# k^T v of the fourth batch placed inside the last block of the second unit's second stage

## The chip, the cores and the metric

The kernel runs on one core of one Trainium2 chip. The time is the device time of that core in microseconds, the median of three runs. A profile comes from one further execution under the hardware profiler. In it PE is TensorE (PEld its weight loads), DVE is VectorE, ACT is ScalarE, POOL is GpSimd and SP is SyncE, which here only issues transfers.

## What is computed

Two stages of a network, one behind the other, in float32 (the weights arrive in a wider type and are folded to float32 on the chip):

```python
# q, k, v: (8 batches, 8 heads, 576, 64)
kv  = np.einsum('bhsd,bhse->bhde', k, v)
out = np.einsum('bhsd,bhde->bhse', q, kv)
rms = np.sqrt(np.mean(out * out, axis=-1, keepdims=True) + 1e-06)
x   = (out / rms * g_norm)            # then (B,H,S,D) -> (4608, 512)

# w_in: (512, 2048), w_out: (2048, 512)
h = x @ w_in
r = np.maximum(h, 0.0)
g = s * (r * r) + b
out = g @ w_out                       # (4608, 512)
```

## The kernel before

The 4608 rows are cut into 36 chunks of 128 rows and nine units of four chunks. A unit u goes through a first stage (x @ w_in, then the squared relu) and a second stage (g @ w_out). Both stages use Strassen-like schemes: seven products of halves in place of eight, with sums of the operands made by VectorE. They are named after the bank that they fill and their number: x1, z2, x6, y7, x5, x3, y4. From the third unit on (u = 2), part of the first stage is split once more; `small(i, pair, ...)` (line 882) are its quarter-size products.

Units count from 0 in the code, batches too. The "second unit" is u = 1, the "fourth batch" is b = 3.

Everything is in an order written out by hand: each engine runs its instructions in the order in which the Python code emits them, and waits only on semaphores for data and buffers. Attention of the next unit is laid between the products of the present one. It comes in steps: `turn` transposes q on VectorE, `product` multiplies it with `bd_kv`, `back`, `square`, `row_sum`, `norm` and `turn_x` finish it. `bd_kv` holds k^T v of two batches, one in each of two buffers (`bd_kv[b % 2]`).

`kv_product(b, beside)` (lines 365 to 400) makes k^T v of one batch: for each of two halves, nine steps of four 64x64 products (in the trace 144 matmuls in all), which fall into the four quadrants of the array; then ScalarE copies the results into `bd_kv[b % 2]`. With `beside` true the results go into one bank of the tag "z" and one of the tag "y" of the pool `ps_f`, which the unit's own products use as well. Without it they go into the two banks of the pool `ps_t` with the tag "t", in which attention's `product` writes.

The table `kv_due` says in which unit a batch's k^T v is made: b = 2 in u = 1, b = 3 in u = 2, b = 4 in u = 3 and so on. k and v of that batch come through a ring of 14 slots in SBUF, `w_sb`, that also carries the weights of the second stage and of the split first stage. `pump()` issues the next loads of one long list on SP's queue as long as slots are free; `used(...)` marks entries as read, frees the slots from the front of the list, and pumps. A load waits, on SP, until the last reader of its slot is done, and the loads behind it wait with it. At the end of u = 1 the list holds: the weights of products 5, 3 and 4 of its second stage (four slots each), then eight loads of k and v for u = 2 (line 114), ten loads of split weights for u = 2 (line 1075), and then the second stage's weights of u = 2 (line 1089).

The second stage of u = 1 is a list of 14 functions, `mm2(1)`, called in a loop (line 1814). Each is one product for one half of the rows; `product(i, j, ...)` (line 1113) runs eight blocks, one matmul of the program each; the trace records each float32 matmul as two, with a weight load each, so that the halves j = 0 and 1 together are 32 recorded 128x256 matmuls. The last two are y4(0) and y4(1). Behind each function run the steps that the dictionary of `side_of` (line 1628) names for its index: parts of the attention for u = 2, and loads of q.

The first stage of u = 2 is `run` in `mm1_deep(u)` (line 947). It calls `at(n)` between products; `sides(u, A, B)` (line 1728) says what stands at each n. Its beginning is:

```python
x1(0)
at(2)
x1(1)
sums_of_x()
small(2, 0, 1, 2)
x6(0)
at(4)
```

`at(2)` is the turn of q for the first attention pair (VectorE) and, in units 2 and 5, `kv_product` with `beside`. `at(4)` is that pair's `product` with `bd_kv`, the first reader of the fourth batch's k^T v. `sums_of_x` is four subtractions on VectorE. `small(2, 0, 1, 2)` is four matmuls into the bank of the tag "x" of `ps_a` (sx_ps) and four into a "z" bank.

Of the kernel before, what the change touches and what calls it, by code (L numbers as in the profile page):

```python
# [17 lines left out]
def kernel(  # L18
# [47 lines left out]
    NP = H // 2  # L66
    KC = DM // P
    FC = DF // P
# [22 lines left out]
    def matmul(o, lhsT, rhs, start, stop):  # L91
        nc.tensor.matmul(o, lhsT=lhsT, rhs=rhs, start=start, stop=stop, skip_group_check=True)  # L92
# [166 lines left out]
    def add(o, a, b):  # L259
        nc.vector.tensor_tensor(out=o, in0=a, in1=b, op=ALU.add)  # L260
# [98 lines left out]
    def warm(n):  # L359

        ps = ps_f.tile([P, 2, TB], FP32, name="warm_ps", tag="z", bufs=1)
        for _ in range(n):
            matmul(ps[:, 0, :P], ident, ident, True, True)

    def kv_product(b, beside=False):

        if beside:
            ps = [  # L370
                bank_of("kv", tag, bufs).rearrange("p b (m d) -> p (b m) d", d=D)[:, :2]
                for tag, bufs in (("z", 1), ("y", 2))
            ]
        else:
            ps = [ps_t.tile([P, 2, D], FP32, name="kv_ps", tag="t") for _ in range(2)]
        for i in range(2):
            if b == 0:
                warm((18, 7)[i])
            kv = [kv_in.pop((b, 2 * i + l)) for l in range(2)]
            for j in range(R):  # L380
                for l in range(2):
                    for r in range(2):
                        rows = slice(r * HB, r * HB + HB)
                        nc.tensor.matmul(  # L384
                            ps[r][(r ^ l) * HB : (r ^ l) * HB + HB, i, :],
                            lhsT=kv[l][0][rows, j, :],
                            rhs=kv[l][1][rows, j, :],
                            start=(j == 0),
                            stop=(j == R - 1),
                        )  # L390
        for r in range(2):
            rs = slice(r * HB, r * HB + HB)
            for l in range(2):
                cs = slice((r ^ l) * HB, (r ^ l) * HB + HB)
                to = bd_kv[b % 2][rs, l:NP:2, rs].rearrange("p i (c e) -> p i c e", c=KC)
                src = ps[r][cs].rearrange("p i (e c) -> p i c e", c=KC)
                if b == 0 and l == 1:
                    nc.vector.tensor_copy(out=to, in_=src)
                else:
                    nc.scalar.copy(to, src)  # L400
# [237 lines left out]
    def bank_of(key, tag, bufs=2):  # L638
        bank[key] = ps_f.tile([P, 2, TB], FP32, name=f"{tag}_ps", tag=tag, bufs=bufs)
        return bank[key]  # L640
# [407 lines left out]
    kv_due = {(b // 2 * R + b % 2 * 4) // 4 - 1: b for b in range(2, B)}  # L1048
# [43 lines left out]
    def used(*keys):  # L1092

        done.update(keys)
        while held and held[0] in done:
            held.pop(0)
        pump()
# [5 lines left out]
    def mm2(u, step=None, side={}):  # L1103
# [6 lines left out]

        st = {}

        def product(i, j, ps, first):
            for f in range(FC // 2):
                s, b = divmod(f, 2)
                w2 = W2_AT[i][:, f] if u == 0 else ring[u, i, f // 4][:, :, f % 4]
                matmul(
                    ps, ga[G_OF[i], s][:, b, j * P : j * P + P], w2,
                    first and f == 0, f == FC // 2 - 1,
                )  # L1120
            if u > 0 and j == 1:
                used((u, i, 0), (u, i, 1))

        def plus_of(o, ps, other, copy=nc.scalar.copy):
# [173 lines left out]
            plus_of(rows("o1", j)[:, HN:], st["x", j], None if u == 1 else st["o1", j][:, HN:])  # L1298
            store("o1", j, 4 * u + j)

        def y4(j):
            product(4, j, st["y", j], False)
            add(rows("o2", j)[:, :HN], st["y", j], st["r2", j])
            store("o2", j, 4 * u + 2 + j)

        def seq(fn, *more):
            def run():
                fn()
                for m in more:
                    m()  # L1310
            return run
# [28 lines left out]
        if u == 1:  # L1340
            return [
                seq(lambda: x1(0), lambda: parts_of_w(1)),
                seq(lambda: x1(1), s2),
                seq(lambda: z2(0), lambda: parts_of_w(2)),
                seq(lambda: z2(1), s4),
                seq(lambda: x6(0), lambda: parts_of_w(6)),
                lambda: x6(1),
                seq(lambda: y7(0), lambda: parts_of_w(7)),
                lambda: y7(1),
                seq(lambda: x5(0), lambda: parts_of_w(5)),  # L1350
                lambda: x5(1),
                seq(lambda: x3(0), lambda: parts_of_w(3)),
                lambda: x3(1),
                seq(lambda: y4(0), lambda: parts_of_w(4)),
                lambda: y4(1),
            ]

        def slot(j, k):
# [163 lines left out]
    blocks = [i for s in range(NS) for i in (2 * s, NU + 2 * s)]  # L1522
# [45 lines left out]
    turn, take, product, square, root, norm, turn_x = zip(*(attention(c) for c in range(4)))  # L1568
# [59 lines left out]
    def side_of(A, B, sums, u):  # L1628

        if u == 0:  # L1630
            return {
                6: [A["turn"], lambda: kv_product(1)],
                8: [A["product"], A["back"], A["square"]],
                9: [A["row_sum"], B["turn"]],
                10: [A["norm"], partial(loads, 2, 0), A["turn_x"], A["scale"], B["product"], B["back"], B["square"]],
                11: [B["row_sum"], B["norm"]],
                12: [B["turn_x"], B["scale"], lambda: [fn() for fn in sums_w_in(0)]],
                13: [sums],
            }
        pieces = []  # L1640

        def ask(n):
            if n == 0:
                pieces.extend(load_q(14))
            for piece in pieces[4 * n : 4 * n + 4]:
                piece()

        return {
            0: [A["scale"]],
            1: [B["turn"]],  # L1650
            4: [B["product"], B["back"], B["square"]],
            5: [B["row_sum"]],
            6: [B["norm"]],
            7: [partial(ask, 0)],
            8: [B["turn_x"], B["scale"], partial(ask, 1)],
            9: [partial(ask, 2)],
            10: [partial(ask, 3)],
            11: [sums],
        }

    def loads(u, i):
# [62 lines left out]
    def y4(a):  # L1724
        for name in ("y4", "y4_square", "x3_s1", "x3_s3"):
            a[name]()

    def sides(u, A, B):

        first, second = {}, {}
        kv = []
        if u in kv_due:
            kv.append(lambda: kv_product(kv_due[u], u > 1))
            kv.append(lambda: used(*((u, "kv", (n, m)) for n in range(NP) for m in range(2))))
        q = {half: [partial(loads, u + 2, half)] for half in range(2)}
        if u == 1:
            for s in range(1, NS - 1):
                first[((0, 1), (0, 3))[s - 1]] = list(sums_w_in(s))  # L1740
            of = [half for key in DEEP for half in sums_of_w_in(key)]
            first.update({
                (1, 0): of[:2],
                (1, 1): of[2:3],
                (1, 2): of[3:4],
                (1, 3): [*kv, of[4]],
                (2, 0): [A["turn"], of[5]],
                (2, 1): [A["product"], of[6]],
                (2, 2): [A["back"], of[7]],
                (2, 3): [A["square"], of[8]],  # L1750
                (3, 0): [of[9], A["row_sum"]],
                (3, 2): [A["norm"], A["turn_x"]],
                (3, 3): [lambda: [load() for load in load_q(12, rest_on=nc.sync)]],
            })
            return first, second
        if u + 1 == U:
            return first, second
        first = {
            2: [A["turn"], *(kv if u in (2, 5) else [])],
            4: [A["product"], *(kv if u not in (2, 5) else [])],  # L1760
            5: [A["back"], A["square"], B["turn"]],
            6: [A["row_sum"]],
            7: [A["norm"]],
            8: [A["turn_x"]],
            10: [B["product"], *q[0]],
            11: [B["back"], B["square"], A["scale"]],
            12: [B["row_sum"]],
            13: [B["norm"]],
            14: [B["turn_x"]],
            15: q[1],  # L1770
        }
        second = {1: [B["scale"]]}
        second[5], second[6] = [[lambda n=n: x_sums(u + 1)[n]()] for n in range(2)]
        return first, second

    for u in range(U):
        A, B = pairs_of(u + 1) if u + 1 < U else (None, None)
# [3 lines left out]
        else:  # L1781
            if u == 1:
                loads(2, 1)
            first, at_second = sides(u, A, B)
# [89 lines left out]
```

## Time and profile before

| | us |
|---|---|
| median of three runs (902.97 to 903.10) | 903.06 |
| the profiled execution's own time | 905.29 |
| its span, first to last instruction | 903.5 |
| TensorE busy in the span | 889.9 |
| VectorE, ScalarE, GpSimd busy | 683.1, 345.4, 262.5 |
| mean granted TensorE clock | 0.999 |

The profiled execution is another execution than the timed ones and took 2.2 us longer than their median. A busy time is the union of an engine's instructions, without the time in which it issues transfers or waits. "Issue" as a releaser means that the engine waited for nothing that the profile shows. The stretch that the change touches lies between 228 us, where y4(0) of the second unit begins, and 250 us, in the first stage of the third.

The transfers there, by the profile's account of issues (KB each, median us from issue to landing), from 195 to 262 us:

```profile
w<-sub POOLq DMA_DIRECT2D x24, 256.0 KB, 6.4
w_sb<-w SPq DMA_DIRECT2D x17, 256.0 KB, 6.1
w_sb<-in_k_dram SPq DMA_DIRECT2D x4, 288.0 KB, 4.8
w_sb<-in_v_dram SPq DMA_DIRECT2D x4, 288.0 KB, 7.0
```

The first row is weight sums that go back to DRAM on GpSimd's queue, the second the loads into the ring, the last two k and v of the fourth batch.

### The profile page before, as it was taken

The page shows a single profiled execution, that of the slowest core. Times are in us where ns is not written, and L with a number is a line of the kernel's source. Part 1 is how long each engine was busy: PE and PEld are TensorE (multiplying, and loading weights), DVE is VectorE, ACT ScalarE, POOL GpSimd, SP SyncE. Part 2 cuts the span into 40 slices and gives each one's busy share as a digit, 9 for nine tenths or more (in the row PEclk, how much of TensorE's full clock was granted, in tenths as well). Part 3 has the DMA queues.
Part 4 walks back from the last instruction along what each step waited for, and adds up shares of the span by engine and source line. Part 5 has one row for each costly group of instructions (what it writes and reads, how often), then busy time and mean ns, then how long its engine had stood idle before and what let it go on. Part 6 is the DMA issues. An engine that isn't in the chain of part 4 may idle for free.

```text
span 903.5 us, 19737 instructions
## 1 busy us (share of the span) xinstructions
PE 889.9 (98%) x7662; PEld 823.2 (91%) x7662; DVE 683.1 (76%) x1321; ACT 345.4 (38%) x584; POOL 262.5 (29%) x493
## 2 busy tenths in 40 slices
PE   6999999999999999999999999999999999999998
PEld 6888888888889998999899989999999989999998
DVE  2898687785587976788678867887779787974695
ACT  2887124522166104630365026701660056204610
POOL 2028057015743024701571037403530300021000
PEclk9999999999999999999999999999999999999999
DMA  9897739449933995389646983498439811992186
GB/s 243 304 356 224 202 80 292 155 104 361 340 117 93 309 311 165 81 262 319 204 98 193 311 274 73 142 323 266 138 107 305 290 54 59 300 305 73 59 279 189
DMA packets 121805, 188.77 MB, mean 209 GB/s; under 512 B 25456, under 2 KB 43248, under 8 KB 121712
## 3 DMA queue, kind: packets, MB, share of 16 engines
q1 hardware_dynamic: 101744, 161.65, 55.1%
q0 software_dynamic: 16512, 23.63, 9.4%
q10 hardware_dynamic: 3456, 2.23, 1.0%
q8 instruction: 61, 1.00, 0.5%
q14 instruction: 32, 0.26, 0.1%
HBM read 160.70 MB, written 26.74 MB: 207 GB/s over the span
## 4 chain that ended last, share of the span: by engine, by line
PE 93%; DVE 3%; DMA 1%; issue 1%; ACT 0%; SPq 0%; POOL 0%; DVEq 0%
PE x_ps L92 46%; PE y_ps L92 25%; PE z_ps L92 10%; PE sx_ps L92 6%; PE st_ps L92 2%; PE y_ps L552 2%; DMA kv_sb<-in_v_dram 1%; PE z_ps L384 1%; PE kv_ps L384 1%; PE y_ps L384 0%; DVE xT L596 0%; DVE xn L585 0%; DVE xs L263 0%; DVE q_sb L564 0%; DVE qT L540 0%
## 5 line engine op out<-in xcount | busy, mean ns | idle before, releaser
L1665 POOL DMA_DIRECT2D q_sb<-in_q_dram x296 | 167.1, 573 | 86.1 <-issue 44.1
L1248 POOL DMA_DIRECT2D out_dram<-o x120 | 59.5, 503 | 360.3 <-issue 211.5
L92 PE MATMUL x_ps<-w_sb,sub 128*128 128x128 f32 x1176 | 148.5, 275 | 0.0
L92 PEld LDWEIGHTS x_ps<-w_sb,sub 128*128 128x128 f32 x1176 | 139.8, 192 | 0.0
L651 ACT ACTIVATE a<-a,b_col,s_col 128x512 f32<-128x512 f32 x144 | 117.1, 813 | 25.6 <-DVE a L654 17.5
L848 ACT COPY a<-x_ps 128x512 f32<-128x512 f32 x28 | 16.3, 582 | 244.3 <-PE x_ps L92 244.2
L92 PE MATMUL y_ps<-xs,wb 128*128 128x256 f32 x416 | 98.5, 380 | 0.0
L92 PE MATMUL x_ps<-xs,ws_raw 128*128 128x256 f32 x384 | 91.1, 380 | 0.1
L92 PEld LDWEIGHTS y_ps<-xs,wb 128*128 128x128 f32 x416 | 76.3, 190 | 9.1 <-issue 0.2
L92 PE MATMUL x_ps<-xT,wa 128*128 128x256 f32 x360 | 84.3, 382 | 0.1
L92 PEld LDWEIGHTS x_ps<-xs,ws_raw 128*128 128x128 f32 x384 | 70.0, 190 | 8.7 <-ACT r L725 0.5
L92 PEld LDWEIGHTS x_ps<-xT,wa 128*128 128x128 f32 x360 | 66.5, 190 | 10.7 <-ACT a L944 1.7
L944 ACT ACTIVATE a<-a 128x512 f32<-128x512 f32 x112 | 69.5, 621 | 5.5 <-DVE a L267 5.5
L92 PE MATMUL x_ps<-w_sb,a 128*128 128x128 f32 (+1 forms) x432 | 64.9, 298 | 0.0
L92 PE MATMUL y_ps<-w_sb,a 128*128 128x128 f32 (+1 forms) x416 | 62.1, 295 | 0.0
L92 PEld LDWEIGHTS x_ps<-w_sb,a 128*128 128x128 f32 x432 | 58.4, 192 | 2.9 <-issue 0.4
L92 PEld LDWEIGHTS y_ps<-w_sb,a 128*128 128x128 f32 x416 | 56.1, 192 | 2.1
L260 DVE TENSOR_TENSOR r<-sx_ps,a 128x256 f32<-128x256 f32 x84 | 35.1, 418 | 24.6 <-PE sx_ps L92 24.1
L260 DVE TENSOR_TENSOR r<-x_ps,o 128x256 f32<-128x256 f32 (+1 forms) x84 | 29.6, 353 | 28.5 <-PE x_ps L92 27.8
L92 PE MATMUL y_ps<-w_sb,sub 128*128 128x128 f32 x392 | 49.5, 275 | 0.0
L92 PE MATMUL z_ps<-w_sb,a 128*128 128x128 f32 (+1 forms) x352 | 46.9, 280 | 0.0
L263 DVE TENSOR_TENSOR a<-a,a 128x512 f32<-128x512 f32 x72 | 46.7, 682 | 0.1
(222 smaller groups left out, 1604.3 us busy)
## 6 DMA issues: line engine op xcount, KB each, us to landing
w_sb<-w SPq DMA_DIRECT2D x413, 256.0 KB, 4.7
w_sb<-w SPq DMA_DIRECT2D x14, 512.0 KB, 8.5
w<-sub POOLq DMA_DIRECT2D x28, 256.0 KB, 6.3
out_dram<-o POOLq DMA_DIRECT2D x112, 64.0 KB, 4.1
w_sb<-in_k_dram SPq DMA_DIRECT2D x24, 288.0 KB, 4.5
w_sb<-in_v_dram SPq DMA_DIRECT2D x24, 288.0 KB, 4.5
w_raw<-in_moe_w_in_dram SPq DMA_DIRECT2D x6, 1024.0 KB, 7.2
q_sb<-in_q_dram POOLq DMA_DIRECT2D x160, 32.0 KB, 3.1
```

The lines of the kernel that those rows point to most:

```text
L92: nc.tensor.matmul(o, lhsT=lhsT, rhs=rhs, start=start, stop=stop, skip_group_check=True)
L260: nc.vector.tensor_tensor(out=o, in0=a, in1=b, op=ALU.add)
L263: nc.vector.tensor_tensor(out=o, in0=a, in1=b, op=ALU.subtract)
L384: nc.tensor.matmul(ps[r][(r ^ l) * HB : (r ^ l) * HB + HB, i, :], lhsT=kv[l][0][rows, j, :], rhs=kv[l][1][rows, j, :], start=(j == 0), sto ...
L552: nc.tensor.matmul(ps[l][32 * p : 32 * p + 32, r, lo:hi], lhsT=bd_kv[b % 2][rows, p, at : at + 32], rhs=st["qT"][rows, p, lo:hi], start=Tr ...
L651: nc.scalar.activation(t, t, AF.Identity, scale=s_col, bias=b_col)
L848: nc.scalar.copy(g_tile("a11", s), st["x", s])
L944: nc.scalar.square(ga[name, s], ga[name, s])
L1248: queues[s % 2].dma_start(out=view[b, jj, :, cols], in_=st[name, j][s * w : s * w + w, cols])
L1665: load()
```

## The change

`product` takes a range of blocks. The last entry of the second stage's list of u = 1, y4(1), becomes two: its first four blocks, and then its last four with the add and the store. The list so has 15 entries. Behind the first of the two, at index 13, stand the steps `kv_of(2)`: k^T v of the batch that is due in unit 2, b = 3, and the marking of its ring slots as used. They are taken out of `at(2)` of unit 2; unit 5 keeps its own there. `beside` is now true only for u > 2, so this k^T v goes into the two banks of `ps_t`. The marking of product 4's ring slots stays behind its last block. On SP, GpSimd and VectorE the order of the instructions is as before; on ScalarE the four copies into `bd_kv` stand ahead of the copy of x1(0) of unit 2 instead of behind it.

```diff
-        def product(i, j, ps, first):
-            for f in range(FC // 2):
+        def product(i, j, ps, first, blocks=range(FC // 2)):
+            for f in blocks:
                 s, b = divmod(f, 2)
...
-            if u > 0 and j == 1:
+            if u > 0 and j == 1 and f == FC // 2 - 1:
                 used((u, i, 0), (u, i, 1))
...
-        def y4(j):
-            product(4, j, st["y", j], False)
+        def y4(j, blocks=range(FC // 2)):
+            product(4, j, st["y", j], False, blocks)
             add(rows("o2", j)[:, :HN], st["y", j], st["r2", j])
             store("o2", j, 4 * u + 2 + j)
...
                 seq(lambda: y4(0), lambda: parts_of_w(4)),
-                lambda: y4(1),
+                lambda: product(4, 1, st["y", 1], False, range(FC // 4)),
+                lambda: y4(1, range(FC // 4, FC // 2)),
...
             11: [sums],
+            13: kv_of(2),
...
+    def kv_of(u):
+
+        if u not in kv_due:
+            return []
+        return [
+            lambda: kv_product(kv_due[u], u > 2),
+            lambda: used(*((u, "kv", (n, m)) for n in range(NP) for m in range(2))),
+        ]
+
     def sides(u, A, B):
...
-        kv = []
-        if u in kv_due:
-            kv.append(lambda: kv_product(kv_due[u], u > 1))
-            kv.append(lambda: used(*((u, "kv", (n, m)) for n in range(NP) for m in range(2))))
+        kv = kv_of(u)
...
-            2: [A["turn"], *(kv if u in (2, 5) else [])],
+            2: [A["turn"], *(kv if u == 5 else [])],
```

## The prediction

> **What bounds the kernel now.** I read the engine totals first, then TensorE's own waits, then the chain of waits around the moved step, then the transfers at the one place where the chain has a hole.
>
> The page, engine totals, clock and DMA rows (busy us, share of the span, instructions; then tenths in 40 slices; then the queue that brings TensorE's instructions: packets, MB, share of 16 engines):
>
> ```profile
> PE 889.9 (98%) x7662; PEld 823.2 (91%) x7662; DVE 683.1 (76%) x1321; ACT 345.4 (38%) x584; POOL 262.5 (29%) x493
> ...
> PEclk9999999999999999999999999999999999999999
> DMA  9897739449933995389646983498439811992186
> ...
> q8 instruction: 61, 1.00, 0.5%
> ```
>
> TensorE is busy 889.9 of 903.5 us at full clock. The chain of waits gives it 93%. No other engine can be the bound over the whole; what a move on TensorE can win is only what TensorE idles. Its waits, all of them over 0.4 us:
>
> ```profile
> PE kv_ps L384 <- DMA kv_sb<-in_v_dram: 3.5, 2, 2.5
> PE z_ps L92 <- issue: 1.6, 1, 1.6
> PE xT_ps L491 <- DVE xn L473: 1.5, 1, 1.5
> PE warm_ps L92 <- POOL ident masks.py:199: 1.4, 1, 1.4
> PE x_ps L92 <- DVE qT L439: 0.8, 1, 0.8
> ```
>
> Four of the five belong to the first 22 us (first loads, first attention). One does not: 1.6 us, a single gap, at a first-stage product of the later units, ended by nothing that the profile shows. The chain from 235.6 us on (start, us, what) shows where it is:
>
> ```profile
> 235.62 1.73 PE x_ps L92 x8
> ...
> 239.62 1.93 PE x_ps L92 x8
> 241.55 0.44 PE sx_ps L92 x4
> 241.99 0.11 PE z_ps L92
> 242.11 1.61 issue
> 243.72 0.60 PE z_ps L92 x3
> 244.32 1.73 PE x_ps L92 x8
> ...
> 247.88 0.45 PE z_ps L92 x4
> ```
>
> 235.62 is x1(0) of the third unit, then k^T v of the fourth batch (237.35 to 239.62, the lines left out), x1(1), then small(2, 0, 1, 2), whose four z matmuls are cut after the first. A semaphore would have held the first of the four, which opens the bank. Four such matmuls take 0.45 us at 247.88; here they take 0.11 + 1.61 + 0.60 = 2.32. The hole costs 1.87 us, not 1.61: the three behind it start from an empty array.
>
> The DMA rows for 241.2 to 241.4 us:
>
> ```profile
> q1 hardware_dynamic: 28, 0.06, 75.4%
> q8 instruction: 1, 0.02, 35.6%
> ```
>
> One instruction packet starts here; 35.6% of 16 engines over 0.2 us is 1.14 us, so it ends near 242.4, and TensorE goes on at 243.72. The one before starts between 214 and 215; from 215.5 to 241 there is none; the next start between 247 and 248 and between 253 and 254. 61 packets of 16.4 KB for 15,324 recorded TensorE instructions is 251 each (256 with the sequencer's waits). So I read the hole as TensorE out of instructions.
>
> **What the Trainium skill says.** "Runtime: NRT & Kernel Launch", Instruction fetch mechanics: instructions come in 16 KiB blocks of 256, the next fetched while the present one runs, and the crossing is mostly hidden. The packets agree in size; the hole is the crossing that isn't hidden. "DMA: Bandwidth & Descriptors", Queues, rings and completion order: each DMA engine goes round its queues packet by packet, so a fetch stands behind kernel traffic; here the DMA share is 1.04 from 237.3 to 239.6 us and 1.05 from 239.6 to 242.1. "TensorEngine Tiling (Array Packing)", Key Properties: changing the tiling drains the engine. The trace agrees mildly: weight loads idle 0.33 us ahead of k^T v.
>
> **Why this crossing.** k^T v is 144 matmuls and 144 weight loads in about 2.3 us, some 125 instructions a us; 128x256 products use 16 in 1.73 us, 9.2 a us. The missing block begins 288 + 16 + 8 + 2 = 314 instructions after the start of k^T v, so the block ahead of it begins at number 58 of k^T v. The sequencer runs ahead of the array: it handles the waits of k^T v from 233.3 on, with the matmuls from 237.28, some 35 instructions early. So I put the request at number 25 or so: 237.28 + 0.2 = 237.5 us. Packet end 242.4: 4.9 us later; resumed 1.3 us after that: 6.2 in all. The 4.4 us to 241.94, where the second z matmul was due, do not cover that.
>
> **The change, part by part.** Product: y4(1) is cut after 4 of 8 blocks, k^T v goes between, and x1(0) and x1(1) become neighbours. Same 144 matmuls, same number of tiling switches (one into k^T v, one out, between 128x256 products in both places). Nothing is added on TensorE: 0 us; bounds -0.1 to +0.1 from the 0.33 us of idle weight loads, taken as 0.
>
> Instruction supply: y4(1)'s second half (16 instructions) and x1(0) (16) now run behind k^T v. The block edges stay within a few instructions (at most three waits more), as the same instructions precede the z matmuls. k^T v starts at 228.56 + 24 x 0.216 = 233.75, say 233.8. The request falls at number 57: 233.8 + 0.45 = 234.25. The z matmul is still due at 241.94. That leaves 7.7 us where the last fetch took 6.2. Transfers issued by SP at 233.93 land 4.7 us later; a fetch like that is served by 239 and usable by 240.3. DMA is no fuller: share 0.91 from 233.81 to 237.28. The hole goes: -1.87 us. Bounds: 0 (another hole of the same size) to -1.9.
>
> Loads of k and v: they are not moved, and land before need. The last pair is issued at 227.02 and 227.44 and lands 4.2 and 4.8 us later, 232.3; the second half of k^T v, which reads it, starts at 233.8 + 1.1 = 234.9. 2.6 us spare: 0.
>
> SP queue: ring slots. The two loads that wait for y4(1) (235.66 and 236.03) move by 2.3 us to about 238; the eight behind them, which waited for k^T v, no longer do, but queue behind: 238.47 becomes about 238.8. Their first readers (weights of small(4, 0)) run near 270, the second stage later still: 0.
>
> ScalarE: the four copies into bd_kv (4 x 0.26 = 1.05 us) run near 236.2 instead of 239.66, in an idle stretch of 8.26 us. VectorE: the add of y4(1) goes from 235.66 to about 238.0; queued behind it are the turn of q (1.24) and four sums of x (0.42 each), 3.3 us to 238.99 before, less 0.22 of a DMA wait that will be over: done by 241.2, and the next add needs its product at 242.0. Spare 0.8 us: 0. If that cover fails, the products at 244 have 3 us more. GpSimd: the store of y4(1) starts after 246 in any case. Banks: attention's two banks were last used near 205 and are next wanted near 244: the added self-wait is long satisfied. The wait of small(2, 0, 2) on the bd_kv copies, done by 240.8, is dropped: 0.
>
> What is late next: nothing for TensorE up to the end; the chain behind 244.3 is products back to back, so the whole 1.87 us reaches the end.
>
> **The sum.** The profiled execution took 905.29 us, 1.79 outside its span of 903.5; less 1.87 it is 903.42. The median is 903.06, 2.2 us below the profiled execution. The difference carried over gives 903.06 - 1.87 = 901.19 us, about 901.2. The doubt is in those 2.2 us: the timed runs may have less of a hole, or none.
>
> **Rivals.**
> (a) The timed runs have no hole, and the change then moves nothing: 903.1. For it: the 2.2 us. Against: the three runs agree within 0.13 us, which a fetch that barely arrives would not give, and the lag comes from the kernel's own traffic.
> (b) The hole in the timed runs is larger. If the fetch lagged 6.5 us to packet end where the profile has 4.9, it costs 3.5 us, all of it saved: 899.6; half that excess: 900.4. For it: the block behind, requested near 239.4, came at 248.3, 8.9 us later.
> (c) Slower: the fetch, requested at 234.25, catches that 8.9 us lag, because the loads bunched at 238 stand ahead of it. 234.25 + 8.9 + 1.3 = 244.45 against 241.94: 2.5 us, 2.8 with the refill. With the hole of before in the timed runs that is 904.0; without it 905.9. It decides from a lag over 6.4 us to packet end. Against: the bunch is issued 3.7 us after the request.
> (d) The last v pair lands late: it would need 7.5 us instead of 4.8; the same stretch has one load of 7.7. The wait would be 0.2 us. Inside (c) and the forecast's margin.
>
> **How the numbers follow.** A difference under 0.2% (1.8 us) can't be told from none; the forecast stands on that edge, at 0.21%. Forecast 901.2, own range 900.8 to 901.6: 0.62, of it 0.35 below 901.25 and 0.27 above. (a) 0.14, no change. (b) 0.12, faster. (c) with (d) 0.12: 0.09 slower, 0.03 unchanged. Faster 0.47, same 0.44, slower 0.09. The range runs from 900.4 to 903.4: the forecast, (a) and part of (b).
>
> **What would show it.** Right: no gap over 0.5 us on TensorE from 230 to 260 us, the instruction packet that started at 241.3 now starting before 239.5, k^T v at 233.8 with no wait for in_v_dram, x1(1) near 239.56 as before, everything behind it 1.9 us earlier, and copies into bd_kv near 236.2. Wrong: an issue gap near 242 or later, a DMA wait in k^T v, or the sums of x on VectorE holding a product between 242 and 250. If the hole is gone in the profile and the median stays, (a) holds.

## The result and the profile after

| | before, us | after, us |
|---|---|---|
| median of 20 runs each | 903.65 (902.50 to 904.47) | 901.86 (901.63 to 902.45) |
| the profiled execution's own time | 905.29 | 901.80 |
| its span | 903.5 | 900.0 |
| TensorE busy in the span | 889.9 | 890.9 |

The ratio of after to before is 0.9982, 95% interval 0.9976 to 0.9989: 1.6 us less, between 1.0 and 2.2. With 20 runs in place of three, the median of before is 903.65 where it was 903.06.

The page of the kernel after, engine totals (busy us, share of the span, instructions) and the queue that brings TensorE's instructions:

```profile
PE 890.9 (99%) x7662; PEld 824.0 (92%) x7662; DVE 683.1 (76%) x1321; ACT 345.2 (38%) x584; POOL 262.2 (29%) x493
...
q8 instruction: 61, 1.00, 0.4%
```

The counts of instructions on every engine, and of instruction packets, are those of before. TensorE's idle time fell by 4.5 us. Its busy time rose by 1.0 us: the first warming matmuls, which the change does not touch, took 5.80 us in the profile of before and 6.86 in that of after. TensorE's largest waits in the kernel after (us in total, times, longest):

```profile
PE xT_ps L491 <- DVE xn L473: 1.5, 1, 1.5
PE warm_ps L92 <- POOL ident masks.py:199: 1.4, 1, 1.4
PE kv_ps L384 <- DMA kv_sb<-in_v_dram: 1.0, 2, 0.7
PE x_ps L92 <- DVE qT L439: 0.6, 1, 0.6
```

The row "z_ps <- issue: 1.6" is gone. What is left stands in the first attention, at the start. The timeline of TensorE around the change in the kernel after (start, us, engine, line, output and inputs, instructions):

```profile
227.29 5.34 PE L92 MATMUL y_ps<-w_sb,a 128*128 128x256 f32 x24
232.56 2.34 PE L384 MATMUL kv_ps<-w_sb 64*64 64x64 f32 x144
234.84 1.99 PE L92 MATMUL y_ps<-w_sb,a 128*128 128x256 f32 x8
236.67 3.62 PE L92 MATMUL x_ps<-xT,wa 128*128 128x256 f32 x16
240.12 0.61 PE L92 MATMUL sx_ps<-xT,wa 128*128 128x128 f32 x4
240.56 0.61 PE L92 MATMUL z_ps<-xT,wa 128*128 128x128 f32 x4
241.01 1.89 PE L92 MATMUL x_ps<-xs,ws_raw 128*128 128x256 f32 x8
```

The 24 matmuls of the first row are the 16 of y4(0) and the first half of y4(1). Then come k^T v into `kv_ps`, which are attention's banks, the second half of y4(1), and x1(0) and x1(1) in one row. The four z matmuls stand in one row of four, 0.45 us ahead of the next product; before, they were cut after the first.

The span fell by 3.5 us, and only 1.88 of it is the hole. At the k^T v of the later batches, all of after runs 3.15 us ahead of before (340.37 to 337.23, 435.82 to 432.67, 526.08 to 522.92, 627.25 to 624.09). At the first z matmul, ahead of the hole, the lead is 1.27 (241.83 to 240.56). Nearly all of the 1.27 comes from the start, in code that the change does not touch: the first k^T v waited 3.5 us for v in the profile of before and 1.0 in that of after, and 1.06 us of that went again into the longer warming matmuls. 3.15 less 1.27 is 1.88. The last 0.35 us lie in the output stores at the end. The 1.27 and the 0.35 are differences between two single executions; the three further profiles of before (below) have spans of 902.4 to 902.6, one further profile of after 900.3.

### The profile page after: what moved, and what is told of

The parts are those of the page before. It is cut to its first block, busy times and chain, and to the rows that moved or that the text cites. A ratio compares the mean times of both kernels' runs of the same rounds, so it can differ in the third digit from the quotient of the medians.

```text
span 900.0 us, 19734 instructions
## 1 busy us (share of the span) xinstructions
PE 890.9 (99%) x7662; PEld 824.0 (92%) x7662; DVE 683.1 (76%) x1321; ACT 345.2 (38%) x584; POOL 262.2 (29%) x493
## 5 line engine op out<-in xcount | busy, mean ns | idle before, releaser
L848 ACT COPY a<-x_ps 128x512 f32<-128x512 f32 x28 | 16.3, 582 | 238.9 <-PE x_ps L92 238.9
```

The lines of the kernel that those rows point to most:

```text
L848: nc.scalar.copy(g_tile("a11", s), st["x", s])
```

## The experiments

In what follows a block is the 256 instructions that one packet brings, its edge is the first instruction of the next block, the request is the moment (by the prediction's count) at which the sequencer begins the block ahead and so asks for the next one, and the lag runs from the request to the end of the packet.

The theory: TensorE ran out of instructions at the edge of a block of 256, because the packet with the next block came late, while k^T v used up instructions faster than anything else. The place of k^T v relative to that edge decides. The rivals: the gain comes from the other banks; it comes from the new place as such; the timed runs have no hole and the gain is something else. Unless another is named, ratios are to the kernel before on the same chip, with 33 of its runs (median 904.06) for the first four experiments and 42 (median 903.73) for the next four.

### Banks alone, and place alone

Before, with the fourth batch's k^T v in its old place but in attention's banks:

```diff
-            kv.append(lambda: kv_product(kv_due[u], u > 1))
+            kv.append(lambda: kv_product(kv_due[u], u > 2))
```

> The kernel before with one part of the change alone: k^T v stays in the third unit behind x1(0), but goes into attention's two banks. Theory (a hole in TensorE's instruction supply, set by where k^T v stands in the instruction stream): the stream is the same to within a few instructions, so the hole stays, 1.3 to 2.2 us near 242 us, ended by issue, and the time is within 0.1% of the kernel before. Rival (the z bank, or its copies on ScalarE, held the z matmuls): the hole goes and the time falls by 0.18%, to a ratio near 0.998.

Measured: 904.04 (902.21 to 906.37), ratio 0.9996 [0.9985, 1.0006]. TensorE's waits in this kernel keep the row:

```profile
PE z_ps L92 <- issue: 1.6, 1, 1.6
```

After, with the banks of before (`u > 2` in `kv_of` back to `u > 1`):

> The other part alone: k^T v between the halves of y4(1), but in the unit's banks (one z, one y) as before. Theory: as the changed kernel, no gap over 0.5 us on TensorE from 225 to 260 us, ratio 0.998 (0.9975 to 0.9990). Rival (the banks matter): the hole at the z matmuls stays, ratio 1.000.

Measured: 902.02 (901.57 to 902.90), ratio 0.9978 [0.9969, 0.9988], and no such row. The banks alone change nothing that these runs can tell (0.1% either way); the place alone gives the gain.

### The same gain with nothing moved

Before, with 32 recorded instructions fewer ahead of k^T v. In the warming matmuls at the start, 16 of the first 18 become 8 of double width; each float32 matmul of the program is two recorded matmuls and two weight loads, so 8 fewer are 32 fewer.

```diff
-        for _ in range(n):
+        two = ident.unsqueeze(1).to_broadcast((P, 2, P))
+        wide = 8 if n == 18 else 0
+        for _ in range(wide):
+            matmul(ps[:, 0].rearrange("p (a n) -> p a n", a=2), ident, two, True, True)
+        for _ in range(n - 2 * wide):
             matmul(ps[:, 0, :P], ident, ident, True, True)
```

> The kernel before, nothing moved; 16 of the 18 warming matmuls at the very start are made as 8 of twice the width, so that 32 TensorE instructions fewer stand ahead of everything else. Theory: the edge of the instruction block falls 32 instructions later, among the products of attention, near 244.2 us; the fetch asked for near 237.7 has 6.5 us where it took 6.2, so the hole shrinks from 1.9 us to between 0 and 0.6, at another instruction (attention's product, not the z matmul), and the ratio is 0.998 to 0.999. Rival (the order of work around x1(0), z and k^T v makes the hole): it stays at the second z matmul with 1.6 us, ratio 1.000.

Measured: 902.16 (901.70 to 902.89), ratio 0.9977 [0.9970, 0.9985]. k^T v stands behind x1(0), as before, and starts at 236.28; there is no TensorE wait at all from 225 to 262 us. So the gain does not need the new place: another distance, counted in instructions, between k^T v and the block's edge is enough.

That the hole hangs on the instruction's number and not on the work there shows in the counts. The windows view gives each engine's busy time and, in brackets, its instructions from the start to the hole; the first two brackets are TensorE's matmuls and weight loads. The kernel before, up to 242.1 us:

```profile
0.00:242.10 242.10, 234.16 (x1863) 202.81 (x1863) 176.61 (x280) 106.81 (x176) 89.36 (x166) 1.00 0.75 238
```

The kernel with 24 instructions more ahead (described below), whose hole is in x1(1), up to 238.9 us:

```profile
0.00:238.90 238.90, 232.15 (x1863) 201.11 (x1864) 176.61 (x280) 105.79 (x174) 87.39 (x162) 1.00 0.75 239
```

3726 and 3727 recorded instructions, in two different products.

### Fewer transfers around the fetch

Before, with k^T v and its place relative to the edge unchanged. The loads that queue on SP behind product 4 of the second unit are held back: its slots are marked as used only behind x6(0), behind a small store to a scratch tile in DRAM that makes SP wait for the copy of x6(0).

```diff
+        def hold():
+            nc.sync.dma_start(out=hold_dram, in_=st["r2", 0][:, 0, :P])
+            used((1, 4, 0), (1, 4, 1))
...
-            if u > 0 and j == 1:
+            if u > 0 and j == 1 and (u, i) != (1, 4):
                 used((u, i, 0), (u, i, 1))
...
-            2: [A["turn"], *(kv if u in (2, 5) else [])],
-            4: [A["product"], *(kv if u not in (2, 5) else [])],
+            2: [A["turn"], *(kv[:1] if u == 2 else kv if u == 5 else [])],
+            4: [A["product"], *([lambda: late["hold"](), *kv[1:]] if u == 2 else kv if u != 5 else [])],
```

> The kernel before, nothing moved on TensorE; the twelve loads of SP's queue that follow the last use of product 4's weights (two of them issued at 234 to 235 us, the rest from 235.7 on) are held back until x6(0) has been copied, near 246 us, by one small store of that copy ahead of them. Theory (the instruction fetch lags because these loads fill the DMA engines): with SP's queue quiet from 234 on the fetch asked for near 237.5 is in by 240, and the hole shrinks from 1.9 us to under 0.4; ratio 0.998 to 0.9987. Rivals: the lag of the fetch is fixed, or the hole is no fetch at all: it stays at 1.6 us, ratio 1.000. If the held loads are themselves late, a wait for a DMA shows at sx products near 258 us.

Measured: 902.18 (901.57 to 902.76), ratio 0.9973 [0.9961, 0.9984]. The hole is gone. SP's part of the timeline shows the pause in its loads (start, us, line, transfer, number):

```profile
227.48 0.80 SPq L1083 DMA_DIRECT2D w_sb<-w  x2
243.60 0.32 SPq L857 DMA_DIRECT2D hold<-r  x1
244.02 2.29 SPq L1083 DMA_DIRECT2D w_sb<-w  x4
```

The DMA rows of the same kernel from 234 to 237.1 us (queue, packets, MB, share of 16 engines):

```profile
q0 software_dynamic: 269, 0.63, 62.5%
```

Only GpSimd's queue moves data, at a share of 0.62, where the prediction read 1.04 from 237.3 to 239.6 us. The packet runs from 237.10 to 238.41, and the z matmul after the edge was due at 240.57. The kernel has one wait that no other profile lists, for a late load at 888.4 us ("x_ps <- DMA w_sb<-w: 0.7"); whether the hold is behind it is not shown.

### The edge put back behind the new place

The kernel after, with more instructions ahead of its k^T v, so that the next edge comes as soon behind it as it did in before. Three tries. The first cut 14 of the first 18 warming matmuls into two halves of 64 columns, 56 recorded instructions more:

```diff
+        narrow = 14 if n == 18 else 0
+        for _ in range(narrow):
+            for h in range(2):
+                matmul(ps[:, 0, h * HB : h * HB + HB], ident, ident[:, h * HB : h * HB + HB], True, True)
+        for _ in range(n - narrow):
```

> The changed kernel, nothing moved; 14 of the 18 warming matmuls at the start are made as two of half the width, so that 56 TensorE instructions more stand ahead. Theory: the block edge now falls at most a few instructions behind k^T v, at the start of y4(1)'s second half, and the fetch is asked for when k^T v begins (232.5 us in that profile); with the 4.5 us to packet end and 1.3 us more that the fetch there took, TensorE goes on near 238.3 where it would at 234.8: a hole of 3 to 4 us ended by issue right behind k^T v, and the kernel is slower than the changed one by that, near 905, ratio 1.001 to 1.003 against the kernel before. Rival: no hole, since all work stands where the changed kernel has it: ratio 0.998.

Measured: 912.38 (911.36 to 913.09), ratio 1.0087 [1.0071, 1.0103]. A miss on both counts. Most of the time went at the start, where the narrow matmuls took 14 us in place of 6.9 for the 128 columns of after. Two rows from the start of TensorE's timeline:

```profile
1.36 14.02 PE L92 MATMUL warm_ps<-ident 128*128 128x64 f32 x64 [1.36 <-POOL ident masks.py:199]
...
21.98 0.21 PE L388 MATMUL kv_ps<-kv_sb 64*64 64x64 f32 x1 [1.86 <-issue]
```

The second row is a new hole of the kind looked for, in another k^T v: TensorE idles for 1.86 us ahead of the last matmul of the first batch's. A packet ran there from 19.64 to 20.62, and TensorE went on 1.36 us after its end. Up to the end of that k^T v the kernel lost 8.0 us against after: 7.16 in the warming matmuls and 1.86 in this hole, less 1.02 of waits for v that after has there. Another 1.1 us are lost up to the second batch, where the clock is lower for a while: in three windows of 2 us from 22 us on the mean granted clock is 0.86, 0.50 and 0.79, which is 3.4 us at half clock, and 128-column matmuls start every 0.21 us where after has 0.11.

The k^T v of the fourth batch has next to no hole behind it: the second matmul after it starts 0.46 us behind the first, where 0.32 is usual, so 0.14 us is lost. I put the request for the missing block at 241.7 us, by the prediction's way of counting; the packet ran from 242.09 to 243.05, so the lag was 1.35 us in all, and that matmul started 1.43 us after its end. At the request the DMA rows (241.5 to 242 us) show one queue at work:

```profile
q0 software_dynamic: 50, 0.16, 85.4%
q1 hardware_dynamic: 1, 0.00, 0.1%
```

The second and third try cut the second stage's product 1 of the second unit, columns in two halves, in four blocks (32 instructions more) or in seven (56 more); here the last:

```diff
+                if (u, i) == (1, 1) and 1 <= f <= 7:
+                    for q in range(2):
+                        matmul(
+                            ps[:, q * P : q * P + P], ga[G_OF[i], s][:, b, j * P : j * P + P],
+                            w2[:, q], False, f == FC // 2 - 1,
+                        )
+                    continue
```

> The changed kernel, nothing moved; eight such splits, 32 instructions more ahead, which puts the block edge where the kernel before had it against k^T v: 26 instructions behind its end, here in x1(0), near 237.7 in the changed kernel's profile. Theory: the fetch, asked for near 232.8, takes 4.5 us to its end and 1.3 more if SP's loads of 232.7 and 233.3 are ahead of it, so a hole of 0.5 to 1.5 us comes back in x1(0) and the gain over the kernel before falls from 0.2% to between 0.03 and 0.15%. If the fetch gets in ahead of those two loads there is no hole, and the ratio is 0.998. Rival (it is the place of the work that counts): no hole, 0.998.

Measured: 902.27 (901.81 to 902.93), ratio 0.9976 [0.9965, 0.9986]. A miss in size: at the edge, in x1(0), one matmul starts 0.43 us behind the one before it where 0.22 is usual, so 0.2 us is lost. The packet ended at 236.88, 3.8 us after the request, and the matmul at the edge was due at 238.09. From the start of k^T v to the edge are 314 recorded instructions, as in before, and yet the loss is 0.2 us and not 1.9. So the distance alone does not decide: the work in between lasted 0.5 us longer here, and the fetch was 1 to 2 us quicker than in the profiles of before. By its time this run does not tell the theory from its rival, which also expected 0.998.

The expectation of the third try names the first one "e4":

> The changed kernel with 56 instructions more ahead, by fourteen such splits, in place of the warming matmuls cut in e4, which cost 8.5 us at the start. Theory, with what e4 showed: no hole behind this k^T v, because the fetch is asked for before SP's two loads; but one of about 1.1 us at the k^T v of the sixth batch near 433 us and 0.1 near 525, as in e4; ratio near 0.9985 to 0.9995. Rival (e4's loss was all from its start): no hole anywhere, ratio 0.998.

Measured: 903.81 (903.01 to 905.08, 21 runs), ratio 0.9998 [0.9991, 1.0005]. The whole gain is given back. As expected, it is not lost behind the fourth batch's k^T v but at the sixth's, in another unit. TensorE's waits:

```profile
PE y_ps L384 <- issue: 1.0, 1, 1.0
```

From the matmul ahead of that k^T v to the one behind it are 3.84 us, where 2.58 is usual: 1.25 us. Against after the loss is 0.9998 less 0.9982 of 903.7, 1.45 us, each ratio uncertain by some 0.6 us; what makes up the other 0.2 I did not find. At the same k^T v the profile of the first try lost 1.1 us (a gap of 0.8); that of the second lost 0.4 two products behind it (a gap of 0.2). The counts up to that hole, in the kernel with 56 instructions more (to 436.2 us):

```profile
0.00:436.20 436.20, 429.50 (x3732) 386.87 (x3732) 329.51 (x589) 177.51 (x299) 155.74 (x291) 1.00 0.72 228
```

and in the one with the narrow warming matmuls (to 444.9 us):

```profile
0.00:444.90 444.90, 438.35 (x3732) 395.14 (x3732) 329.45 (x589) 177.67 (x299) 155.86 (x291) 1.00 0.70 223
```

Again one number. With the sequencer's waits counted in, this edge is 3840 or 3841 instructions, by the profile taken, behind the one of before's hole: 15 blocks of 256 are 3840. And in the profile of the first try the hole at the start stands 3328 instructions ahead of the edge behind the fourth batch's k^T v: 13 blocks of 256. So none of the three tries brought a hole of before's size back at this k^T v, but where holes of 0.8 us and more came instead, at other k^T v, they stand whole blocks away, to within one instruction.

### A little more ahead of the old place

Before, with the same cut in three blocks of the second unit's product 1 (24 instructions more):

> The kernel before, nothing moved; six matmuls of the second unit's x1, 50 us ahead, are made as two of half the width, which puts 24 more TensorE instructions ahead of k^T v at 0.1 us. Theory: the block edge falls right behind k^T v, near 239.8, and the fetch is asked for as k^T v begins; with the 6.2 us that it took, TensorE goes on near 243.5: the hole grows from 1.9 to between 2.8 and 4.2 us and stands ahead of x1(1) or in it, ratio 1.001 to 1.0025. Rival: the hole stays with its z matmul, 1.6 us, ratio 1.000.

Measured: 903.71 (902.24 to 906.35), ratio 0.9992 [0.9985, 1.0000]. TensorE's waits:

```profile
PE x_ps L92 <- issue: 0.4, 1, 0.4
```

The hole moved into x1(1) as expected, but the profile has it at 0.4 us only (0.6 us are lost, from the starts of the matmuls). The profiled execution is the fastest of all 19 (902.24), so it probably shows this hole at its smallest. The packet in it ran from 236.70 to 237.58, some 1.7 us after the request, not 4.9; in the slower runs it was probably later, but no profile shows one.

### Before and after profiled again

Three more single profiles of before, and one of after, together on one chip:

> The kernel before again, for one more profile, to see whether the hole differs from execution to execution. Theory: it is there each time, between the first and second of the four z matmuls, 1 to 4 us, and the execution's time follows it (the timed executions of before spread over 902.5 to 906.3 us, those of kernels without the hole over about 1 us). Rival: the hole is of one size, 1.6 us, and the spread has another cause.

> The changed kernel again, for one more profile. Theory: no gap over 0.5 us on TensorE from 225 to 260 us, k^T v within 0.3 us of 232.6 against the first product of the second unit's y4, time 901.6 to 902.5. Rival: a hole that comes and goes, so that some executions of the changed kernel have it.

Measured: before 904.14, 904.38 and 904.23, after 902.04 with no hole. TensorE's waits of the three, one after the other:

```profile
PE z_ps L92 <- issue: 1.5, 1, 1.5
```

```profile
PE z_ps L92 <- issue: 2.3, 1, 2.3
```

```profile
PE z_ps L92 <- issue: 1.4, 1, 1.4
```

All of them stand between the first and the second z matmul of `small(2, 0, 1, 2)`. With the first profile and the one with exchanged banks these are five holes of 1.4 to 2.3 us in five executions. The times of these executions do not follow the holes closely (904.14, 904.38 and 904.23 for 1.5, 2.3 and 1.4 us, 905.29 for the 1.6 of the first profile): the waits for v at the start differ as well, from 0.8 to 3.5 us. The timed runs say the same of the hole in another way: those of before, of the kernel with exchanged banks and of the one with 24 more ahead range over some 4 us (902.2 to 906.5, all taken), and those of after, place alone, fewer ahead, held loads and 32 more ahead over 0.8 to 1.3 us each. A part that varies from run to run goes when the hole goes. Not all of that part need be the hole: of the 108 runs of before, exchanged banks and 24 more ahead in the two series, the 15 from 905.5 us up, and no others, have a mean granted clock of 0.997 or 0.998, and no run of a kernel without the hole has less than 0.999. A stretch of 3.4 us at half clock, as behind the first hole in the profile with the narrow warming matmuls, would lower the mean by 0.002, but no profile of before caught one.

## Why the prediction was right

The forecast was 901.2 us, a gain of 1.87; measured were 901.86 and 1.6 (1.0 to 2.2), or 1.8 between the medians. The absolute figure is 0.7 low, nearly all of it from the base: three runs of before gave 903.06, twenty gave 903.65. So it lies 0.26 above the forecast's own narrow range (900.8 to 901.6) and within the whole range (900.4 to 903.4). That the three runs agreed within 0.13 us, which the prediction held against rival (a), was chance: the twenty spread over 2 us.

Point by point, with 1.19 us added to times of the profile after up to x1(1), for its earlier start as measured at k^T v of the second batch (104.158 against 102.966):

- The product costs nothing to move. From the matmul ahead of k^T v to the one behind it are 2.58 us in both kernels. k^T v starts at 232.56 + 1.19 = 233.75, said 233.8, with no wait for v. Right.
- The fetch comes earlier. The packet ran from 236.58 to 237.54, 237.8 to 238.7 on the clock of before; said: served by 239, and a start before 239.5. The edge was due at 240.57, 3.0 us after its end, 1.6 to 1.8 more than the 1.23 to 1.43 us by which TensorE resumed after the packet's end in the six profiles with a hole at this edge. Right. The packet's row in the kernel after, from 236.4 to 236.8 us (15.0% of 16 engines over 0.4 us is 0.96 us):

```profile
q8 instruction: 1, 0.02, 15.0%
```

- The whole 1.87 reaches the end. 1.88 in the profile, with all later k^T v shifted alike. Right.
- ScalarE and VectorE have the room. Their timelines in the kernel after (the last bracket is the idle time ahead and what ended it):

```profile
234.94 1.08 ACT L400 COPY bd_kv<-kv_ps 64x128 f32<-64x128 f32 x4 [7.08 <-PE kv_ps L384]
```

```profile
236.87 0.42 DVE L260 TENSOR_TENSOR o<-y_ps,or 128x256 f32<-128x256 f32 x1 [2.98 <-PE y_ps L92]
...
239.46 0.42 DVE L263 TENSOR_TENSOR sub<-xT,sub 128x256 f32<-128x256 f32 x1
240.84 0.42 DVE L260 TENSOR_TENSOR r<-sx_ps,a 128x256 f32<-128x256 f32 x1 [0.96 <-PE sx_ps L92]
```

The copies start at 236.1 (said 236.2), the add of y4(1) at 238.1 (said 238.0), the sums are done at 241.1 (said 241.2). Then VectorE waits 0.96 us for TensorE, so it held nothing (said 0.8 to spare). Right.

- SP's loads. The two that wait for y4(1) are issued at 238.05 and 238.4 (said about 238), the eight behind them from 239.2 (said 238.8). Off by 0.4 us, with no reader near.

Of the rivals: (a), no hole in the timed runs, falls with the five profiles and the spread above; the profiled execution at 905.29, from which the doubt came, lies within the 902.5 to 906.5 of the timed runs of before. (b), a larger hole, is half true: one profile has 2.3 us, and the gain between the medians is no larger than one hole. (c) and (d) did not happen: the packet ended 4.5 us after the request, and v was there. The lag of 8.9 us in (b) and (c) was also read too long. It counts from 239.4, but the block that starts at the edge landed only at 242.45, and by the prediction's own rule the next one is asked for when that block begins: from 242.45 to its packet's end at 248.32 are 5.9 us at most, less than the 6.4 that (c) needed.

One thing in the working was too simple, without harm to the forecast: a lag of 4.9 us to the packet's end, carried from one fetch to another. By the same count it was 1.35 us in the kernel with narrow warming matmuls, 1.7 with 24 more ahead, 2.2 with the loads held, 3.8 to 4.5 in the kernel after and with 32 more, and 5.7 in the before with the longest hole. The count of the request is not good to better than half a microsecond: in the kernel with 56 more ahead the packet at the fourth batch started 0.5 us before the counted request. Holding SP's loads back took the lag from 4.8 to 5.7 in five profiles to 2.2 in one, and the hole out of all six timed runs to judge by their times, so those loads are a part of it. They are not all: in the kernel after the DMA rows for the first 1.5 us behind the request show next to nothing but GpSimd's queue, as with the narrow warming matmuls, and the lags are 4.5 and 1.35. What sets it in each case stays open; the request itself is in no record. Three of the expectations, which used a fixed lag, missed in size (0.6, 0.2 and 0.1 us lost, where from 0.5 to over 4 was expected).

That a crossing between blocks is mostly hidden, as the Trainium skill has it ("Runtime: NRT & Kernel Launch", Instruction fetch mechanics), agrees: of the 61 packets of before one goes with a gap that the waits list. The skill also has each DMA engine go round its queues packet by packet ("DMA: Bandwidth & Descriptors", Queues, rings and completion order), from which the prediction took that a fetch stands behind the kernel's own transfers. The run with the loads held agrees with that (a lag of 2.2 us), but not with a fixed price.

No version beat the kernel after. Four others reach it within their intervals (902.02 to 902.27), each by being rid of the same hole.

## What to carry to other kernels

On an engine that is nearly always busy, a gap in the middle of a row of like matmuls, ended by "issue" and with an instruction packet that lands just before work resumes, points to a block of instructions that came late (here the packet landed 1.2 to 1.4 us before work went on, in twelve cases of thirteen). Look then for a burst of short instructions some 256 ahead of it (here 288 in 2.3 us) with the DMA engines full; what removed it here was to put longer instructions between burst and edge, by moving the burst, by shifting the stream by a few tens of instructions, or by holding back loads around the fetch. Any edit that changes the number of instructions moves all later edges as well, so a gain or loss of a microsecond or two may belong to a burst far from the edit: look there before crediting the edit itself.

## What the runs showed of the hardware beyond what was expected

TensorE went on 1.23 to 1.43 us after the end of the late packet in twelve cases, with losses from 0.1 to 2.5 us, and 1.58 us in a thirteenth. A packet of 16 KB itself took 1.0 us in the median of the profile of before (0.9 to 1.5). The wait ahead of it, from the request as I count it, went from 0.4 us, at one edge even less than the count can show, to 4.5 us.

And at the very start the warming matmuls of 128 columns start every 0.21 us at first, and every 0.11 us from a point on that lies between 4.4 and 7.4 us in the profiles. The 56 of 64 columns start every 0.21 us throughout, and so do the eight of 128 columns behind them, up to the end of the row at 15.0 us: halving the columns did not make one shorter, and the quicker rate did not come while they ran. Why is not shown.
